# Four heads per unit and 48 KB per partition in an attention decode kernel that streams its cache

## The chip, the cores and the metric

The kernel runs on one core of a Trainium2 chip. The metric is device time in microseconds (us) of one execution. A "unit" is one step of the main loop: a few heads of one batch element, with all their K and V. A "packet" is what one of the 16 DMA engines moves at a time in the records of the trace: for K and V the part of a load that goes to one partition, 128 packets per load. TensorE's "granted clock" is the share of its full clock that it was allowed. All runs were classed as fast, that is, not in the slower state that some executions fall into. Ratios are the mean time of one kernel's fast runs over that of the other's fast runs of the same rounds, so they are not quite the ratio of the medians quoted beside them.

## The reference

One decode step: a layer norm, attention with one query per head over a cache, an output projection with a residual, then a gated MLP with a second residual. Everything is bfloat16.

```python
B, Sq, D = 4, 1, 640;  Hq, Hkv, Sk, Dh = 32, 32, 4096, 192;  F = 1536
q = (layernorm(x) @ wq)                       # wq 640 x 6144
scores = einsum("bhqd,bhkd->bhqk", q, k_cache) * Dh ** -0.5
o = einsum("bhqk,bhkd->bhqd", softmax(scores), v_cache)
h = x + o.reshape(B, 1, 6144) @ wo            # wo 6144 x 640
out = h + (silu(ln(h) @ w_gate) * (ln(h) @ w_up)) @ w_down
```

K and V are 201 MB each. Nothing of them is used twice, so the work is 424 MB of reading with little arithmetic on each byte.

## The kernel before

Per unit (two heads, one batch element) one load brings K as 128 partitions x 64 positions x 192, that is 24 KB (24576 B) per partition, and another brings V. VectorE multiplies K by the query, TensorE adds up with an identity matrix, VectorE finishes the sum over 16 columns and finds the maximum, ScalarE takes the exponential, TensorE multiplies by V ("pv"). The loads go round six places of 24 KB, all issued by one engine (SyncE, "SP" in the profile) in the order in which they are used.

```python
NS, NPR = 6, 3
ring = [sb(f"ring{j}", [128, T, DH], BF16) for j in range(NS)]      # T = 64: 24 KB per partition
...
def src(c):
    p, b = c[1] // B, c[1] % B
    a = kc if c[0] == "K" else vc
    return a[b, 2 * p:2 * p + 2].rearrange("h (q t) d -> (h q) (t d)", t=T)
...
def load(c):
    n = order[c]
    deps = [lambda: released[chunks[n - NS]]] if n >= NS else ([wq_used] if slot[c] >= 3 else [])
    ...
        landed[c] = [dma("sp", lambda e: e.dma_start(r[:, :, :].rearrange("q t d -> q (t d)"), src(c)), ...)]
...
for c in chunks:
    load(c)
    if c[0] == "V" and c[1] % B == (1 if c[1] < NP - B else B - 1):
        load_wo(c[1] // B)              # 480 KB of wo every fourth unit
```

## Time and profile before

Three runs had a median of 1001.38 us (1000.53 to 1002.6).

| what | value | view |
|---|---|---|
| span of the profiled run | 1000.1 us | page |
| DMA share, 240 to 360 us | 1.00 | windows |
| rate there | 429 GB/s | windows |
| VectorE, TensorE busy | 55%, 66% | page |
| median packet of 24576 B | 915 ns | DMA records of the trace |
| last w_down packet to last output packet | 4.17 us | DMA records of the trace |

Two windows of the kernel before, in the middle of the stream: length, busy time (and instructions) of five engines, TensorE's granted clock, DMA share, GB/s.

```profile
core 0: us, PE busy (x) PEld busy (x) DVE busy (x) ACT busy (x) POOL busy (x), PEclk, DMA share, GB/s
240.00:360.00 120.00, 80.38 (x572) 14.48 (x396) 66.71 (x52) 14.27 (x50) 0.00 (x0) 0.84 1.00 429
360.00:480.00 120.00, 80.13 (x572) 14.56 (x396) 67.49 (x53) 14.27 (x50) 0.00 (x0) 0.83 1.01 430
```

The Trainium skill ("DMA: Bandwidth & Descriptors", section "Where 436 GB/s comes from") gives a ceiling of 435.2 GB/s for the 16 SBUF ports that the DMA engines go through. The trace agrees as far as it goes: 429 to 430 GB/s with no idle time is 1% below that.

The end of the kernel before in the timeline: start, length, engine, line, operation, tiles, and in brackets the idle time before it and what ended it.

```profile
995.82 1.77 PE L532 MATMUL pb<-wd_sb,guT 128*4 128x160 bf16 x48 [1.62 <-DVE guT L528]
997.64 0.33 DVE L535 CAST outsb<-pb 128x160 bf16<-128x160 f32 x1 [1.88 <-PE pb L532]
998.00 0.67 SPq L536 DMA_DIRECT2D out_dram<-outsb  x2
```

The 48 products with w_down start at 995.82 us, and the span ends 4.3 us after that.

### The profile page before, as it was taken

What the parts mean: (1) busy time and instruction counts of PE and PEld (TensorE: products, weight loads), DVE (VectorE), ACT (ScalarE), POOL (GpSimd) and SP (SyncE); (2) the same over time, 40 slices, a digit from 0 to 9 for tenths busy, and PEclk for the clock granted to TensorE, in tenths of its full rate; (3) what the DMA queues carried; (4) which work ended last, traced back from release to release, by engine and by line L of the source; (5) the groups of instructions that cost most, each with busy time, mean ns of one, the idle gap of its engine ahead of it and who ended that gap; (6) DMA issues with size and microseconds to landing.
All of it is one profiled execution on the core that took longest, in us unless ns stands there. A gap on an engine that the chain in (4) does not pass through costs nothing.

```text
span 1000.1 us, 9429 instructions
## 1 busy us (share of the span) xinstructions
PE 661.4 (66%) x4752; PEld 122.6 (12%) x3344; DVE 547.6 (55%) x450; ACT 122.6 (12%) x412; POOL 4.5 (0%) x19
## 2 busy tenths in 40 slices
PE   0676676676676676676677686676676666676686
PEld 0110110111110110110111110110110111110112
DVE  2546556546546546556546546546556546546562
ACT  0110111110110110111010110111011010110112
POOL 1000000000000000000000000000000000000000
PEclk9887887877887887887887877988888887987887
DMA  9999999999999999999999999999999999999996
GB/s 393 427 438 426 427 435 428 426 434 427 427 431 431 425 429 433 430 427 427 433 428 428 432 428 428 427 434 427 428 431 433 425 428 432 428 428 430 431 423 287
DMA packets 21849, 424.90 MB, mean 425 GB/s; under 512 B 2480, under 2 KB 2480, under 8 KB 4912
## 3 DMA queue, kind: packets, MB, share of 16 engines
q1 hardware_dynamic: 21760, 424.29, 99.2%
q8 instruction: 32, 0.52, 0.2%
q14 instruction: 9, 0.07, 0.0%
q10 hardware_dynamic: 48, 0.01, 0.0%
HBM read 424.29 MB, written 0.01 MB: 424 GB/s over the span
## 4 chain that ended last, share of the span: by engine, by line
DMA 65%; PE 23%; DVE 10%; SPq 1%; issue 1%; ACT 0%; ACTq 0%; DVEq 0%
DMA ring<-in_A_k_cache_dram 63%; PE pb L97 13%; DVE prod L319 8%; PE pb L391 3%; DMA xrow<-in_A_x_dram 2%; PE pb L329 2%; DVE sc L335 1%; PE pb L344 1%; PE pb L412 1%; PE pb L353 1%; SPq L304 1%; PE pb L286 1%; DVE msb L340 1%; PE pb L374 0%; PE pb L522 0%
## 5 line engine op out<-in xcount | busy, mean ns | idle before, releaser
L319 DVE TENSOR_TENSOR prod<-ring,qb 128x6144 f16<-128x6144 bf16 x128 | 429.1, 3353 | 303.6 <-DMA ring<-in_A_k_cache_dram 295.9
L97 PE MATMUL pb<-prod,identH 128*128 128x512 f16 x1408 | 434.2, 472 | 0.0
L344 PE MATMUL pb<-identF,msb 128*1 128x128 f32 x128 | 33.9, 362 | 301.7 <-DVE msb L340 301.7
L335 DVE TENSOR_REDUCE sc<-pb 128x32 f32<-128x512 f32 x128 | 88.1, 688 | 112.5 <-PE pb L97 112.5
L358 ACT ACTIVATE negM<-pb 128x2 f32<-128x2 f32 x64 | 11.0, 172 | 713.5 <-PE pb L353 713.5
L391 PE MATMUL pb<-ring,pbuf 128*16 128x384 bf16 x2048 | 94.7, 326 | 0.2 <-ACT pbuf L365 0.2
L365 ACT ACTIVATE pbuf<-sc,negM 64x64 bf16<-64x64 f32 x128 | 73.9, 577 | 3.0
L329 PE MATMUL pb<-prod,identH 128*128 128x512 f16 x128 | 61.3, 479 | 3.2 <-DVE prod L319 3.2
L353 PEld LDWEIGHTS pb<-negMc,ones_row 1*128 1x128 f32 x128 | 19.3, 189 | 280.5 <-issue 258.1
L391 PEld LDWEIGHTS pb<-ring,pbuf 128*16 128x16 bf16 x2048 | 46.4, 89 | 27.5 <-issue 0.5
L344 PEld LDWEIGHTS pb<-identF,msb 128*1 128x1 f32 x128 | 5.5, 81 | 329.0 <-DVE msb L340 329.0
L365 ACT ACTIVATION_READ_ACCUMULATOR pbuf<-sc,negM 64x1 f32 x128 | 41.8, 326 | 0.0
L380 ACT ACTIVATE qb<-pb 128x192 bf16<-128x192 f32 x64 | 21.2, 331 | 103.2 <-PE pb L374 103.2
L374 PEld LDWEIGHTS pb<-qsb,sel 4*64 4x64 bf16 x128 | 6.7, 101 | 163.2 <-issue 161.6
L353 PE MATMUL pb<-negMc,ones_row 1*128 1x2 f32 x128 | 24.8, 261 | 0.7 <-DVE negMc L348 0.7
L412 PE MATMUL pb<-r,orow 128*64 128x4 f32 x384 | 20.0, 231 | 0.6 <-ACT orow L399 0.6
L412 PEld LDWEIGHTS pb<-r,orow 128*64 128x64 f32 x384 | 18.6, 174 | 2.4 <-ACT orow L399 1.0
L374 PE MATMUL pb<-qsb,sel 4*64 4x192 bf16 x128 | 17.2, 265 | 1.0 <-ACT qsb L290 0.6
L348 DVE TENSOR_REDUCE negMc<-pb 1x2 f32<-1x128 f32 x64 | 17.4, 271 | 0.5 <-PE pb L344 0.5
L329 PEld LDWEIGHTS pb<-prod,identH 128*128 128x128 f16 x128 | 12.7, 99 | 32.7 <-issue 28.3
L256 PE MATMUL pb<-mv,quadm 128*128 128x2 f32 x4 | 1.2, 363 | 23.4 <-DVE mv L254 23.4
L340 DVE TENSOR_REDUCE msb<-sc 128x1 f32<-128x64 f32 x64 | 14.1, 220 | 2.2
(61 smaller groups left out, 76.1 us busy)
## 6 DMA issues: line engine op xcount, KB each, us to landing
ring<-in_A_k_cache_dram SPq DMA_DIRECT2D x64, 3072.0 KB, 29.8
ring<-in_A_v_cache_dram SPq DMA_DIRECT2D x63, 3072.0 KB, 22.8
wq_sb<-in_A_wq_dram SPq DMA_DIRECT2D x1, 7680.0 KB, 21.0
wo<-in_A_wo_dram SPq DMA_DIRECT2D x16, 480.0 KB, 23.5
ring<-in_A_v_cache_dram SPq DMA_DIRECT2D x2, 1536.0 KB, 19.3
wg_sb<-in_B_w_gate_dram SPq DMA_DIRECT2D x1, 1920.0 KB, 25.8
wu_sb<-in_B_w_up_dram SPq DMA_DIRECT2D x1, 1920.0 KB, 18.9
wd_sb<-in_B_w_down_dram SPq DMA_DIRECT2D x1, 960.0 KB, 20.8
```

Source lines behind the costliest of these rows:

```text
L97: return e.add_instruction(mybir.InstMatmult(name=e.bass.get_next_instruction_name(), engine=mybir.EngineType.PE, start_tensor_calc=start, ...
L319: tk["tt", n] = op("dve", lambda e: e.tensor_tensor(out=prod[n % NPR][:, :, :], in0=ring[slot[c]][:, h * TH:(h + 1) * TH, :], in1=qbs[i % ...
L329: tk["red", n] = op("pe", lambda e, j=j: (e.matmul if j == 0 else partial(held_matmul, e))(psR[n % 3][:, 0:TH * R], lhsT=identH[:, :], rhs ...
L335: tk["rsum", n] = op("dve", lambda e: e.tensor_reduce(sc[i % 3][:, h * TH:(h + 1) * TH], psR[n % 3][:, 0:TH * R].rearrange("q (t r) -> q t ...
L340: tk["rmax", i] = op("dve", lambda e: e.tensor_reduce(msb[i % 2][:, 0:1], sc[i % 3][:, :], AX.X, ALU.max), [g("rsum", 2 * i), g("rsum", 2 ...
L344: tk["maxT", i] = op("pe", lambda e: e.matmul(psS[0:1, 0:128], lhsT=msb[i % 2][:, 0:1], rhs=identF[:, :], start=True, stop=True), [g("rmax ...
L353: tk["maxB", i] = op("pe", lambda e: e.matmul(psS[:, 128:130], lhsT=ones_row[0:1, :], rhs=negMc[i % 2][0:1, 0:2], start=True, stop=True), ...
L365: tk["exp", i] = op("act", lambda e, hh=hh, r=r: e.activation(out=pbuf[b][r, :, 2 * b + hh], in_=sc[i % 3][r, :], func=ACTF.Exp, bias=negM ...
L374: tk["qb", i] = op("pe", lambda e, hh=hh: e.matmul(psQ[64 * hh:64 * hh + 64, 0:DH], lhsT=sel[32 * n:32 * n + B, b, :], rhs=qsb[32 * n:32 * ...
L380: tk["qbc", i] = op("act", lambda e: e.activation(out=qbs[i % 2][:, :], in_=psQ[:, 0:DH], func=ACTF.Copy, scale=QS), [g("qb", i), g("tt", ...
L391: tk["pv", i] = op("pe", lambda e, t=t, n=n: e.matmul(psO[p % 2][32 * n:32 * n + 4 * B, 0:2 * DH], lhsT=pbuf[b][:, t:t + 2, :].rearrange(" ...
L412: tk["oT", p] = op("pe", lambda e, j=j, hh=hh, k=k: e.matmul(psO[p % 2][64 * hh:64 * hh + 64, OC + B * j:OC + B * (j + 1)], lhsT=orow[p % ...
```

## The change

The intent: fewer and larger transfers. A unit becomes four heads of one batch element, so that K and V come as 48 KB (49152 B) per partition and load. Two places hold K, one holds V (the same 144 KB in all). wo no longer comes in 16 loads along the way, but in two near the end, ahead of the last V. The query broadcasts for all units are made at the start. The last V comes in four pieces. TensorE's stream stays unrolled, as before; a switch (`ROLL`) to roll it into a loop is new and off. The diff, cut to its core:

```diff
+ROLL = False
...
-    T = 2 * cfg.NT
+    T = 4 * cfg.NT
...
-    ring = [sb(f"ring{j}", [128, T, DH], BF16) for j in range(NS)]
+    kslot = [sb(f"k{j}", [128, T, DH], BF16) for j in range(2)]
+    vslot = sb("v", [128, T, DH], BF16)
...
+    def src(a, u):
+        c, b = u // B, u % B
+        return a[b, 4 * c:4 * c + 4].rearrange("h (q t) d -> (h q) (t d)", t=T)
+    def load_k(u):
+        deps = [lambda: tk["tt", u - 2, NQ - 1]] if u >= 2 else ([wq_used] if u == 1 else [])
+        ...
+    VP = [(0, 64), (64, 96), (96, 112), (112, T)]
+    def load_v(u):
+        deps = [(lambda: tk["pv", u - 1]) if u >= 1 else wq_used]
+        ...                                        # whole for u < NU - 1, else in the pieces VP
+    load_k(0)
+    load_k(1)
+    for u in range(NU - 1):
+        load_v(u)
+        if u + 2 < NU:
+            load_k(u + 2)
+    wo_land = []                                   # 12 blocks into K's free place, 4 into prod
+    ...
+    load_v(NU - 1)
+    ...                                            # w_gate, w_up, w_down
...
+    for u in range(NU):
+        pr.step("pe")
+        for k in range(NQ):                        # four quarters of K
+            tt(u, k)
+            if k == NQ - 1 and u >= 1:
+                pv(u - 1)                          # frees the V place
+                tmp(u - 1)
+            red(u, k)
+            ...
+    if ROLL:
+        pr.roll("pe", 2, NU)
```

(Cuts marked with "..."; also cut: the softmax maximum for four heads instead of two, the sums of the exponentials, the transpose of the result per unit, and wo's 14 first products after the loop.)

## The prediction

> **What bounds the kernel now.** The DMA engines. The page's slices show DMA at nine tenths or more in every slice but the last, and the windows view gives a DMA share of 1.00 to 1.01 from 22 to 960 us. VectorE is busy 55% and TensorE 66%. In the timeline the multiplies by K start 14.6 us apart where no wo load lies between (60.57, 75.18, 89.79 us), which is the time of 6.29 MB at 430 GB/s. The Trainium skill ("DMA: Bandwidth & Descriptors", "Where 436 GB/s comes from") puts the ceiling at 435.2 GB/s; the trace agrees, being 1% below. So every byte stays to be moved, and only overhead per packet, gaps, start and tail can change.
>
> **What the change does to the stream.** It moves the same bytes. The trace's DMA records give median packet times: 3840 B 149 ns, 12288 B 464 ns, 24576 B 915 ns, 61440 B 2267 ns. The slope from 24576 to 61440 B is 0.0367 ns per byte, leaving some 14 ns per packet. A 49152 B packet should take 1816 ns instead of 2 x 915: 14 ns saved per pair. 16384 packets of 24 KB become 8192 of 48 KB, over 16 engines: 7 to 8 us saved. wo keeps its 3840 B packets (about 19 us in all either way).
>
> **Compute.** Multiply (3.35 us each, 128 of them), the identity sums, rsum and pv keep their shapes and counts. Fewer maxima, exps and q broadcasts run; per-unit o_t, recip and otm are added. All of it is off the critical path: VectorE needs about 17.5 us of work plus waits of 6 to 10 us for the last identity sum and the maximum, within a unit's 29.1 us.
>
> **One V place.** V(u+1) waits for pv(u), which TensorE reaches after the third sum of the next unit. From K's landing I work out 20 to 23 us until that pv ends; the V load is due 27 us after it, since the K load before it takes 14.5 us. So it is hidden, with 4 to 7 us to spare. Two K places leave more.
>
> **Start.** q's projection ends at 31.1 us, K0 occupies the DMA until about 36 us, so K1 is in time. The 16 q broadcasts (about 9 us on ScalarE) hold the first sums until about 41 us; unit 1's pv comes at about 79 us, when V1 is due: a gap of 0 to 3 us, once.
>
> **Tail.** Before, the last wd bytes land near 995.5 us and the end is 4.6 us later, with compute just as late (wd matmuls start at 995.82). Afterwards V's last piece lands earlier relative to the chain, and wo's products are hidden before it, so perhaps 1 us is gained.
>
> **Sum.** 1001.4 - 7.5 + 1 - 1 = about 994 us: 0.7% faster, within 2%. Range 988 to 1002. Chances: faster 0.03, same 0.93, slower 0.04.
>
> **What would show it.** Packets of 49152 B near 1816 ns; K/V rate about 433 GB/s instead of 430; DMA share near 1.00 in all middle windows; in the DMA queue's waits, V loads waiting for pv and still issued before the previous K transfer ends; VectorE idle mostly for K's landing; start gap below 3 us; the last wd landing about 4 us before the end.
>
> **What would make it wrong.** 48 KB packets running slower than the fit (a different reading pattern in HBM); VectorE, TensorE and the maximum chain adding up to more than 29 us per unit when TensorE's clock falls (a half-clock unit comes to about 30 us by the same sum), so that V's single place stalls the DMA in each of 32 units: 2 us of stall per unit would cost 60 us. A longer start gap would cost a few us.

## More of the kernel before

The next lines are from the page of the kernel before. The first gives busy time of each engine, its share of the span and its instructions; the second is the busy share of the 16 DMA engines in 40 slices, in tenths; the third counts the packets of the instruction queue, their megabytes and their share; the last is the group of the multiplies by K: busy time and mean ns of one, then the idle time ahead of them and what ended it.

```profile
PE 661.4 (66%) x4752; PEld 122.6 (12%) x3344; DVE 547.6 (55%) x450; ACT 122.6 (12%) x412; POOL 4.5 (0%) x19
...
DMA  9999999999999999999999999999999999999996
...
q8 instruction: 32, 0.52, 0.2%
...
L319 DVE TENSOR_TENSOR prod<-ring,qb 128x6144 f16<-128x6144 bf16 x128 | 429.1, 3353 | 303.6 <-DMA ring<-in_A_k_cache_dram 295.9
```

Every slice but the last is nine tenths full of DMA, while no compute engine passes two thirds. The multiplies idle for 303.6 us, nearly always for a K load to land. That is what a kernel bound by its transfers looks like: the engines' shares say nothing of its time, the rate of the DMA does.

## The result

The change made it slightly faster: 995.96 us median (995.51 to 996.49, 4 runs) against 1001.01 us (1000.53 to 1002.6, 4 runs) for the kernel before, ratio 0.9945 with a 95% interval of 0.9931 to 0.9959. By the 2% rule that is "same". The predicted 994.0 us missed by 2 us, inside its range.

The same page lines of the changed kernel:

```profile
PE 581.1 (58%) x4656; PEld 117.8 (12%) x3248; DVE 552.7 (56%) x451; ACT 108.0 (11%) x348; POOL 3.4 (0%) x19
...
DMA  9999999999999999999999999999999999999997
...
q8 instruction: 31, 0.51, 0.2%
...
L403 DVE TENSOR_TENSOR prod<-k,qball 128x6144 f16<-128x6144 bf16 x128 | 426.3, 3351 | 204.4 <-DMA k<-in_A_k_cache_dram 204.4
```

The picture is that of before, with compute still further from mattering: TensorE fell from 661 to 581 us of busy time and the time hardly moved. The multiplies' own time is the same (426.3 us), and their idle time is again spent waiting for K.

The same windows of the changed kernel:

```profile
240.00:360.00 120.00, 71.17 (x562) 13.96 (x380) 71.47 (x54) 11.57 (x40) 0.00 (x0) 0.80 1.00 432
360.00:480.00 120.00, 72.12 (x565) 13.99 (x377) 68.44 (x54) 11.99 (x41) 0.00 (x0) 0.79 1.00 432
```

The share was 1.00 and is 1.00. The rate went from 429 or 430 to 432 GB/s. The gain of the middle is in that number: 0.6% of 930 us of K and V is about 5 us.

The end of the changed kernel:

```profile
989.92 0.92 PE L561 MATMUL pb<-wd_sb,guT 128*4 128x160 bf16 x40 [1.62 <-DVE guT L557]
...
991.17 0.31 PE L561 MATMUL pb<-wd_sb,guT 128*4 128x160 bf16 x8 [0.34 <-DMA wd_sb<-in_B_w_down_dram]
991.53 0.33 DVE L564 CAST outsb<-pb 128x160 bf16<-128x160 f32 x1 [1.67 <-PE pb L561]
991.89 0.67 SPq L565 DMA_DIRECT2D out_dram<-outsb  x2
```

Here 40 of the 48 products with w_down are done before its last piece has landed, and the last eight wait for it. From there to the end of the span it is 2.8 us.

The DMA records of the two traces, added up over sixteen engines, give the parts. The first four rows are sums of packet durations divided by 16, the last two are distances in time.

| part, us | before | after | difference |
|---|---|---|---|
| K and V | 939.05 | 932.95 | -6.10 |
| semaphore packets (4 B) | 1.38 | 0.70 | -0.68 |
| wo (3840 B packets) | 19.37 | 19.87 | +0.50 |
| wq | 18.68 | 18.91 | +0.23 |
| first wq packet to last w_down packet | 993.35 | 988.96 | -4.39 |
| last w_down packet to last output packet | 4.17 | 2.46 | -1.71 |

The last two rows together are the 6.1 us between the two spans (1000.1 and 994.0). The rows above them add to 6.05 us, but the stream became only 4.39 us shorter. Packets overlap a little at their edges, so a sum of durations does not turn into time one to one. The records show it: at times more than 16 packets are under way, and what is above 16 adds up to 4.63 us of sixteen engines before and 2.67 us after. With half the packets of K and V there is less overlap to lose, and these 2.0 us are nearly all that is missing between the sum and the stream.

### The profile page after: what moved, and what is told of

It reads as the page before. It is cut to its first block, busy times and chain, and to the rows that moved or that the text cites. A ratio compares the mean times of both kernels' runs of the same rounds, so it can differ in the third digit from the quotient of the medians.

```text
span 994.0 us, 9003 instructions
## 1 busy us (share of the span) xinstructions
PE 581.1 (58%) x4656; PEld 117.8 (12%) x3248; DVE 552.7 (56%) x451; ACT 108.0 (11%) x348; POOL 3.4 (0%) x19
## 4 chain that ended last, share of the span: by engine, by line
DMA 66%; PE 19%; DVE 13%; SPq 1%; issue 0%; DVEq 0%
DMA k<-in_A_k_cache_dram 60%; PE pb L152 12%; DVE prod L403 12%; PE pb L455 5%; DMA wd_sb<-in_B_w_down_dram 3%; DMA v<-in_A_v_cache_dram 3%; PE pb L411 2%; DVE sc L416 1%; SPq L350 0%; SPq L377 0%; SPq L354 0%; SPq L371 0%; SPq L373 0%; PE pb L425 0%; DVE msb L421 0%
## 5 line engine op out<-in xcount | busy, mean ns | idle before, releaser
L403 DVE TENSOR_TENSOR prod<-k,qball 128x6144 f16<-128x6144 bf16 x128 | 426.3, 3351 | 204.4 <-DMA k<-in_A_k_cache_dram 204.4
L152 PE MATMUL pb<-prod,identH 128*128 128x512 f16 x1408 | 388.2, 433 | 0.0
L411 PE MATMUL pb<-prod,identH 128*128 128x512 f16 x128 | 58.8, 459 | 340.0 <-DVE prod L403 340.0
L455 PE MATMUL pb<-v,pbuf 128*8 128x384 bf16 x2048 | 91.8, 332 | 9.4 <-DMA v<-in_A_v_cache_dram 9.4
L461 ACT ACTIVATE otmp<-pb,mask 128x192 f32<-128x192 f32 x32 | 13.4, 420 | 680.0 <-PE pb L455 680.0
L444 ACT ACTIVATE pbuf<-sc,negM 32x128 bf16<-32x128 f32 x128 | 73.4, 573 | 2.7 <-ACT negM L438 0.2
L455 PEld LDWEIGHTS pb<-v,pbuf 128*8 128x8 bf16 x2048 | 47.2, 87 | 121.8 <-issue 82.7
L444 ACT ACTIVATION_READ_ACCUMULATOR pbuf<-sc,negM 32x1 f32 x128 | 31.7, 248 | 0.0
L480 PE MATMUL pb<-pick,orow 128*64 128x2 f32 x384 | 22.4, 229 | 5.6 <-DVE orow L465 1.0
L480 PEld LDWEIGHTS pb<-pick,orow 128*64 128x64 f32 x384 | 20.5, 175 | 8.1 <-issue 6.4
L434 PE MATMUL pb<-negMc,ones_row 1*128 1x4 f32 x64 | 12.2, 258 | 11.8 <-DVE negMc L429 11.8
L425 PE MATMUL pb<-identF,msb 128*1 128x128 f32 x64 | 12.2, 271 | 5.5 <-DVE msb L421 1.1
L294 DVE BATCH_NORM_STATS2 stats<-xrow 128x6 f32<-128x160 bf16 x1 | 0.3, 327 | 17.6 <-DMA xrow<-in_A_x_dram 17.6
```

What stands on the lines that cost most here:

```text
L152: return e.add_instruction(mybir.InstMatmult(name=e.bass.get_next_instruction_name(), engine=mybir.EngineType.PE, start_tensor_calc=start, ...
L403: op("dve", lambda e: e.tensor_tensor(out=prod[BUF[k]][:, :, :], in0=kslot[u % 2][:, k * QT:(k + 1) * QT, :], in1=qball[:, u, None, :].bro ...
L411: op("pe", lambda e, j=j: (e.matmul if j == 0 else partial(held_matmul, e))(psR[k][:, 0:QT * R], lhsT=identH[:, :], rhs=prod[BUF[k]][:, :, ...
L425: op("pe", lambda e: e.matmul(psS[0:1, XT], lhsT=msb[:, 0:1], rhs=identF[:, :], start=True, stop=True), [g("rmax", u), g("negM", u - 1), p ...
L434: op("pe", lambda e: e.matmul(psS[:, XB], lhsT=ones_row[0:1, :], rhs=negMc[0:1, :], start=True, stop=True), [g("hmax", u), g("negM", u - 1 ...
L444: op("act", lambda e, h=h, r=r: e.activation(out=pbuf[r, :, h], in_=sc[u % 2][r, :], func=ACTF.Exp, bias=negM[r, h:h + 1], scale=alpha, ac ...
```

## The experiments

Theory A: the transfers bind both kernels, and in the stream the change gains the cost that each packet has beyond its bytes; the rest of the gain is in the tail. Theory B: the stream gained from something else that changed with it (wo in one place, fewer broadcasts and maxima, the unit's order), and the packet size is incidental. A second question is how far the one place for V and the compute of a unit are from costing time. Two attempts to do better follow.

### K and V in packets of 24 KB again

Everything else of the change stays. Each load is issued as two, with a semaphore each, and whoever uses it waits for both.

```diff
-        landed["k", u] = dma("sp", lambda e: e.dma_start(
-            kslot[u % 2][:, :, :].rearrange("q t d -> q (t d)"), src(kc, u)), S_k[u % 2], deps)
+        s = src(kc, u).rearrange("q (t d) -> q t d", d=DH)
+        landed["k", u] = [dma("sp", lambda e, n=n: e.dma_start(
+            kslot[u % 2][:, n * T // NSP:(n + 1) * T // NSP, :], s[:, n * T // NSP:(n + 1) * T // NSP, :]),
+            S_k[u % 2][n], deps) for n in range(NSP)]          # NSP = 2; V likewise
```

> The changed kernel, but every K and V load is issued as two loads of 24 KB per partition, and their users wait for both. Theory A, the size of the packets is what the change gained in the stream: packets of 24576 B near 916 ns again, the stream 6 to 7 us longer, time 1001 to 1003 us, ratio to the kernel before 1.000 to 1.002. Theory B, the gain came from the rest (wo in one place, fewer broadcasts and maxima, the last V in pieces): the time stays near 996 us, ratio 0.995.

Measured: 1001.16 us (1000.8 to 1002.06, 5 runs) against 1001.84 us for the kernel before in the same rounds, ratio 0.9993 (0.9979 to 1.0007). The packets' median is back at 914 ns (915 in the kernel before). A window of it:

```profile
240.00:360.00 120.00, 69.59 (x531) 13.24 (x345) 71.44 (x55) 11.58 (x40) 0.00 (x0) 0.80 1.00 430
360.00:480.00 120.00, 71.09 (x533) 13.35 (x356) 68.99 (x53) 11.58 (x40) 0.00 (x0) 0.79 1.00 429
```

The rate is 429 to 430 GB/s, that of the kernel before. With the packet size undone, the gain is gone: from a ratio of 0.9945 to 0.9993, 0.48% or 4.8 us, with an uncertainty of about 2 us from the two intervals. The edit also doubles the number of these loads, but that is not where the time went: in the records the durations of the K and V packets themselves add up to 6.2 us more than in the changed kernel, and the semaphore packets of the added loads to 0.6 us. Theory B expected 0.995. What else the change did to the time is 0.7 us with an uncertainty of 1.4 us.

### K and V in packets of 12 KB

The same edit with `NSP = 4`.

> As e1, with four loads of 12 KB per partition. Theory A: packets of 12288 B near 464 ns, 4 x 464 = 1856 ns for what one packet of 48 KB does in 1821 ns, with three more semaphore packets of 9 ns each per load and engine: 17 + 2 us, time about 1014 to 1016 us, ratio 1.013 to 1.015. Theory B: near 996 us. If the cost came from the number of loads in the queue rather than from bytes per packet, the packets' own durations would not show it and the DMA share would fall.

Measured: 1010.37 us (1010.2 to 1010.55, 5 runs), ratio 1.0084 (1.007 to 1.0098). The window:

```profile
240.00:360.00 120.00, 70.06 (x529) 13.12 (x344) 70.02 (x53) 11.58 (x40) 0.00 (x0) 0.80 1.01 426
```

The direction and the cause are as A has them: the DMA share stays at 1, the rate falls to 426 GB/s, the packets' median is 464 ns. The size was overestimated: 14 us more than the changed kernel, where 18 to 20 had been expected, and the reason is visible in the records. Beside the changed kernel the packet durations add up to 19.8 us more, the stream from the first wq packet to the last w_down packet is only 14.5 us longer; with 24 KB packets the two numbers are 6.6 and 6.0 us. Per additional K or V packet of an engine (504 with 24 KB, 1512 with 12 KB) the stream grew by 11.8 and 9.6 ns. These two figures hold one profiled run each, and a part of them is no cost of packets: engines stood idle for 1.3 and 0.6 us more than in the changed kernel, mostly at the end of the stream, when some have nothing left to do. Without that it is 9.2 ns in both, and by the ratios of all fast runs (4.8 and 13.9 us) 9.5 and 9.2 ns. So a packet costs 9 to 10 ns beyond its bytes, semaphore packets of the added loads included, less than the 14 ns that its duration suggests. The rest goes into overlap: what is above 16 packets at a time adds up to 2.7, 4.7 and 8.7 us with packets of 48, 24 and 12 KB.

### The last V in one piece

```diff
-    VP = [(0, 64), (64, 96), (96, 112), (112, T)]
+    VP = [(0, T)]
```

> The changed kernel, but the last V load comes in one piece instead of four. If the pieces are what made the tail 1.7 us shorter: all 64 products of the last unit come after the landing instead of the last 8, 2 to 4.5 us more in the chain, of which about 1 us is hidden under the waits for wu and wd: 997 to 999.5 us, ratio 0.996 to 0.999. If the tail hangs on the last wd landing alone: 996 us, and the wait of TensorE for wd stays.

Measured: 999.26 us (998.52 to 1000.1, 5 runs), ratio 0.9972 (0.9959 to 0.9986). The lines of its timeline that matter:

```profile
977.25 5.29 PE L455 MATMUL pb<-v,pbuf 128*8 128x384 bf16 x64 [13.64 <-DMA v<-in_A_v_cache_dram]
...
988.72 1.77 PE L551 MATMUL pb<-wg_sb,lnT 128*4 128x384 bf16 x20 [1.90 <-DVE lnT L308]
...
993.70 1.77 PE L561 MATMUL pb<-wd_sb,guT 128*4 128x160 bf16 x48 [1.62 <-DVE guT L557]
...
995.88 0.68 SPq L565 DMA_DIRECT2D out_dram<-outsb  x2
```

All 64 products now start after the landing at 977.25 us and take 5.29 us at a granted clock of 0.50; in the middle of the kernel, at a granted clock of 1.00, the same 64 took 2.77 us. (TensorE had been idle for 13.64 us before; whether that is why the clock was low was not tested.) Everything behind them moves by 4 us, and the products with w_down no longer wait for its landing: compute has become the end of the chain. From the last w_down packet to the last output packet it is 6.56 us instead of 2.46. The pieces are therefore worth 0.27% of the time, 2.7 us, to this kernel, with an uncertainty of about 1.9 us; between the two profiled runs it is 4.0 us. The kernel before, with its last V in two pieces, lay in between at 4.17 us.

### TensorE's stream rolled into a loop

```diff
-ROLL = False
+ROLL = True
```

> The changed kernel with TensorE's stream rolled into a loop, as its own switch does. The instruction queue took 31 packets of 16 KB, in all 33 us of one engine or 2 us of sixteen. If those delay the data: up to 2 us faster, 994 to 996 us, ratio 0.993 to 0.995, with fewer instruction packets. If waits against a register or the loop's branch cost TensorE more than its slack: slower than 996 us, with V loads issued later after K's landing than 17.6 us.

Measured: 994.15 us (993.87 to 995.56, 5 runs), ratio 0.9925 (0.9912 to 0.9939). The instruction queue of its page and a window:

```profile
q8 instruction: 7, 0.11, 0.0%
```

```profile
240.00:360.00 120.00, 72.65 (x581) 14.27 (x400) 71.39 (x54) 11.58 (x40) 0.00 (x0) 0.80 1.00 433
360.00:480.00 120.00, 71.44 (x548) 13.30 (x353) 68.32 (x53) 12.00 (x41) 0.00 (x0) 0.79 1.00 433
```

7 instruction packets instead of 31, 0.44 us of sixteen engines instead of 2.05 us, and the stream is 1.95 us shorter (988.96 to 987.00 us). The expected gain of up to 2 us is there: 1.8 us by the medians, 2.0 us by the ratios, with an uncertainty of about 1.9 us; the second rolled kernel, below, has the same ratio. The rest of it, beyond the 1.6 us of the packets themselves, fits the K and V packets, whose sum fell by 0.8 us: 31 of them took over 1860 ns instead of 62. Of these 62, 28 overlap an instruction packet in time (of the other packets of 48 KB, 8% do), and 27 of the 31 instruction packets have such a slow one beside them. So a fetch seems to stretch a data packet as well.

### Three and five passes of pv

TensorE does the products of P and V of each unit but the last several times. Each pass starts its sums anew, so the result is right, but V's place and the rest of the unit come 5.5 or 11.1 us later.

```diff
-        for t in range(lo, hi, 2):
+        for t in [t for _ in range(3 if u < NU - 1 else 1) for t in range(lo, hi, 2)]:    # 5 in the second run
```

> The changed kernel, but the 64 products of P and V of each unit but the last are done three times over (each pass starts its sums anew, so the result is right). One pass took 2.77 us, so the free of V's place and the rest of the unit come 5.5 us later. In the profile a unit whose K was there already took 22.8 us (81.52 us, first multiply of unit 2, against 58.77 us) against 29.1 us in which the data of a unit arrive, so theory A, compute and the one V place are off the path with over 6 us to spare: 996 to 1000 us, ratio 0.995 to 0.999, the excess being a gap before V1 at the start. If the one V place were already costing the stream: 5.5 us more in each of 30 units, over 1100 us.

> As e5 with five passes: 11.1 us more in each unit, 22.8 + 11.1 = 33.9 us, more than the 29.1 us. Now compute should bound: 3 to 5 us more in each of some 30 units, 1080 to 1145 us, the VectorE no longer waiting for K, DMA share near 0.87. If the load of V alone were the limit (issued 17.6 + 11.1 = 28.7 us after K's landing, due at about 27.5): 1.2 us a unit, about 1035 us, and VectorE would still wait for K's landing.

Measured: three passes 1008.88 us (1007.76 to 1010.18, 4 runs), ratio 1.0077 (1.0062 to 1.0092); five passes 1151.17 us (1146.68 to 1152.96, 4 runs), ratio 1.1488 (1.1463 to 1.1512). Both are above what was expected. Of each, one line of who waited for whom (total us, times, longest), after that of the changed kernel:

```profile
DVE prod L403 <- DMA k<-in_A_k_cache_dram: 204.4, 30, 12.6
```

```profile
DVE prod L403 <- DMA k<-in_A_k_cache_dram: 48.4, 28, 12.9
```

```profile
DVE prod L403 <- DMA k<-in_A_k_cache_dram: 12.6, 1, 12.6
```

With three passes, 170 us of TensorE work were added (5.5 us in 31 units) and 13 us of time came out. VectorE's wait for K shrank from 204.4 to 48.4 us, on average 1.3 us in each unit after the first: the slack is nearly used up. The 13 us are a gap at the start (the engines idle for the equivalent of 3.3 us before 90 us of the span), 1.7 us of gaps later, twice as many instruction packets (62, 2.0 us more) and K and V packets whose sum is 5.5 us longer; 261 of them took over 1860 ns. Most of these lie near an instruction packet or a gap: 119 of the 261 overlap an instruction packet in time (17% of the other packets of 48 KB do), and 141 start within 2.5 us of a moment with fewer than 15 packets under way (3% of the others do). 49 are near neither, and why a restart should be slow was not tested.

With five passes the slack is gone and the wait for K with it (12.6 us, once at the start). A unit takes about 34 us (first multiplies at 230.47 and 264.48 us), as worked out, and the DMA share falls to 0.88 to 0.91 in the windows from 240 to 930 us. The first of them:

```profile
240.00:360.00 120.00, 102.97 (x1507) 36.46 (x1348) 58.67 (x44) 9.13 (x31) 0.00 (x0) 0.93 0.91 380
```

So in the middle of the stream the changed kernel has room for 5.5 us more per unit, with about 1.3 us then left, but not for 11. The prediction's 4 to 7 us was right for the total, though not where it put it: V's next load is issued 17.6 us after K's first multiply, while the K load ahead of it in the queue still has over 10 us to go, and what runs out first is the chain of VectorE and TensorE over the unit (22.8 us where it had not to wait for K). One unit of the changed kernel, from its first multiply through pv and the issue of the V load to the next unit's first multiply:

```profile
899.45 6.63 DVE L403 TENSOR_TENSOR prod<-k,qball 128x6144 f16<-128x6144 bf16 x2 [6.05 <-DMA k<-in_A_k_cache_dram]
...
914.26 2.77 PE L455 MATMUL pb<-v,pbuf 128*8 128x384 bf16 x64
...
917.08 0.33 SPq L350 DMA_DIRECT2D v<-in_A_v_cache_dram  x1
...
928.88 3.36 DVE L403 TENSOR_TENSOR prod<-k,qball 128x6144 f16<-128x6144 bf16 x1 [7.07 <-DMA k<-in_A_k_cache_dram]
```

### V's loads from a second queue

```diff
-            landed["v", u] = [dma("sp", lambda e: e.dma_start(
+            landed["v", u] = [dma(eng, lambda e: e.dma_start(      # "act": ScalarE's queue
...
                 tmp(u - 1)
+                if u < NU - 1:
+                    load_v(u, "act")
```

> The changed kernel with V's loads issued from ScalarE's queue, K's from SyncE's, so that both queues mostly hold packets. If a second queue lets an engine hide the 12 to 14 ns that a packet costs beyond its bytes: up to 6 us faster, 990 us, ratio 0.989. If an engine takes packets one after the other whichever queue they come from: the same 996 us, ratio 0.995. If sharing the rate delays K's or V's landing so that buffers come free late: slower, with a DMA share under 1.00 in the middle.

Measured: 1053.09 us (1049.86 to 1056.89, 5 runs), ratio 1.0509 (1.0493 to 1.0525). A window near the start, in which packets of both queues were under way all the time, and one from the middle:

```profile
86.00:108.00 22.00, 9.75 (x36) 0.30 (x3) 12.69 (x7) 0.55 (x2) 0.00 (x0) 0.76 1.00 430
240.00:360.00 120.00, 72.72 (x504) 13.62 (x320) 67.49 (x52) 11.61 (x40) 0.00 (x0) 0.78 0.94 399
```

With both queues active the rate is 430 GB/s, no more than with one queue (434 in the same window of the changed kernel), so nothing of a packet's cost was hidden. That agrees with the Trainium skill ("DMA: Bandwidth & Descriptors", section "Issuing engines are not separate DMA queues"), which says that transfers from different issuing engines run on the same 16 engines and interleave. Interleaving is what made it slow. The DMA records show packets of K and V in alternation for some 25 us at a time (from 86 to 110 us, for one); the two land together, late, and after that come moments with no packet of either (near 266 and 328 us), since neither place has been freed. This line tells who waited for whom on TensorE:

```profile
PE pb L453 <- DMA v<-in_A_v_cache_dram: 226.4, 30, 15.6
```

In the changed kernel TensorE's wait for V was 9.4 us in all, here it is 226.4 us, and the DMA share in the middle is 0.94. One queue in the order of use is worth about 57 us to this kernel (the difference of the medians).

### Rolled, and wo in packets of 7680 B

An attempt to beat both kernels: `ROLL = True`, and six rows of wo per partition instead of three, with the transposed result laid out to match (24 small products per unit instead of 6).

```diff
-            wo[...].rearrange("(p q j) n -> q p (j n)", q=128, j=3)), sem(f"s_wo{lo}"), deps)
+            wo[...].rearrange("(p q j) n -> q p (j n)", q=128, j=6)), sem(f"s_wo{lo}"), deps)
...
-                    psL[64 * s:64 * s + 64, lo:lo + 2], lhsT=orow[:, j:DH:3], rhs=pick[:, s:4:2],
+                    psL[32 * s:32 * s + 32, lo:lo + 1], lhsT=orow[:, j:DH:6], rhs=pick[:, s:s + 1],
```

> An attempt to beat both kernels: the changed kernel with TensorE's stream rolled (e4) and wo laid out with six rows per partition instead of three, so that its packets are 7680 B instead of 3840 B. From the packets' times, 2 x 153 ns become 292 ns: 14 ns x 1024 / 16 = 0.9 us. Expected 993 to 994 us, ratio to before 0.991 to 0.993, about 1 us under e4. TensorE does 24 small products instead of 6 per unit, some 1.5 us more, which is within the unit's slack; if it is not, the time rises above e4's.

Measured: 993.51 us (993.29 to 993.77, 5 runs), ratio 0.9923 (0.9909 to 0.9936). It beats both kernels given, but not clearly the rolled kernel above: 0.9923 and 0.9925 lie well within each other's intervals. In the records, packets of wo and of the same size in w_down take 21.32 us instead of 22.06, and the stream is 0.4 us shorter. The 0.9 us that was expected of wo is not confirmed in time.

## Why the prediction was right

The prediction was inside its range and in the right class; the sum was 2 us too favourable. Point by point:

- **What binds.** Right. The DMA share is 1.00 in the middle of both kernels. The change took 80 us of busy time off TensorE and the time fell by 5 us; the packets put back to 24 KB took back 4.8 us of that.
- **The packet's cost.** The mechanism was right, shown by the series 48, 24 and 12 KB with only the split of the loads changed (ratios 0.9945, 0.9993, 1.0084). The size was off: "7 to 8 us saved" became 4.8 us in time and 6.0 us of stream in the profiled runs. The packets did take what was predicted (1819 ns median against 1816), but a packet's duration overlaps its neighbours', and 9 to 10 ns of the 14 ns count. This term was 2.7 us too favourable, more than the whole miss. That the sum came within 2 us is in part luck: the start and the tail, below, gave 0.9 and 0.7 us back.
- **wo "about 19 us in all either way".** Nearly: 19.37 became 19.87 us, and wq's packets also took 0.23 us more. Both were taken as zero.
- **The start gap, "0 to 3 us, once".** The gap was there at the first V of the second unit and cost 0.13 us; 1 us had been put into the sum. With three passes of pv it grew to 3.3 us, which shows it is the wait that was meant.
- **The tail, "perhaps 1 us is gained".** Right in kind, 1.71 us in the profiled runs. The run with the last V in one piece shows that it needs the pieces: without them the tail is 4.1 us longer, and the end no longer hangs on the landing of w_down. How much of the 1.71 us comes from four pieces instead of two, and how much from hiding wo's products, was not tested.
- **The one V place.** Hidden, as said. V's load was issued about 18 us after K's first multiply, earlier than the 20 to 23 us worked out, since only the first of a unit's four sums ran slowly (4.6 us in the unit shown above, 2.8 us each for the others). The danger named at the end was real but more than 5.5 us per unit away, as the two runs with more passes show.

## What to carry to other kernels

When every slice is full of DMA and the rate is within 1 or 2% of the ceiling, expect larger transfers to win back only a fixed cost per packet: count the packets per engine that the change saves and multiply by the 9 to 10 ns measured here for packets of 12 to 48 KB (here 496 of K and V per engine, and 5 us of 1000). Before any such change look at what else goes over the same engines: TensorE's own instructions were worth about 2 us here, for one switch. At the end of a stream, split the last transfer that a long chain hangs on, so that only a small piece of compute follows the landing, and keep the loads on one queue in the order of use.

## What the Trainium skill lacked or had wrong

- "DMA: Bandwidth & Descriptors" (section "Rules for kernel authors") advises 128 partitions and at least 1 MiB per DMA for the most bandwidth. The K and V loads compared here, of 6, 3 and 1.5 MiB, meet that, and they still differ: 432, 429 to 430, and 426 GB/s in the same window. The section "Why small descriptors are slow (HBM only)" names a fixed overhead of about 3 cycles per packet and treats it as a matter of small ones; no figure is given for large packets issued from SyncE. The runs show 9 to 10 ns per packet and engine at 12 to 48 KB.
- "Runtime: NRT & Kernel Launch" (section "Instruction fetch mechanics") says that each engine's sequencer fetches instructions in blocks of 16 KiB over its own DMA queue; the traces agree on the blocks (31 packets of 16384 B, about 1057 ns each, 1.7 times what a K packet takes for as many bytes). It also gives branches as a reason why kernels prefer unrolling. It does not say that the fetch takes time from data: in this kernel, full of DMA, rolling TensorE's loop left 7 packets and gained about 2 us (0.9945 to 0.9925, uncertain by nearly as much; the stream of the profiled run is 1.95 us shorter).
- "DMA: Bandwidth & Descriptors" (section "Issuing engines are not separate DMA queues") says that a second issuing engine saves only the issuing time. It lacks the harm: with V on a second queue the two streams shared the rate, and the time rose by 5.7% against the changed kernel (1.0509 to 0.9945).
